# Reordering the second pass of the first batch in a fused attention and maxout-FFN kernel: left-over scores first, products on zeros, one AV moved

## The chip, the cores and the metric

The kernel runs on one core of one Trainium2 chip. The metric is device time in microseconds; the time before is the median of 11 runs, 325.95 us (323.8 to 327.2).

## What is computed

Attention with a relative position bias (the bias depends only on the distance of query and key and on the head), and after it a feed-forward network that takes the maximum of three products:

```python
# B, H, S, D = 8, 8, 576, 64;  d_model, d_ff = 512, 768
scores = scale * np.matmul(q, k.transpose(0, 1, 3, 2)) + bias
scores = scores - np.max(scores, axis=-1, keepdims=True)
attn = np.exp(scores)
attn = attn / (np.sum(attn, axis=-1, keepdims=True) + 1e-09)
x = np.matmul(attn, v)          # then (B * S, H * D) = (4608, 512)
h = np.maximum(np.maximum(x @ w1, x @ w2), x @ w3)
out = h @ w_out
```

## The kernel before

**Tiles.** Two heads make a pair, four pairs (`hp` = 0 to 3) a batch. Of 576 queries and keys, 512 are handled in four tiles of 128, and the left-over 64 of both heads of a pair together make one more tile. A pair's scores are computed transposed, keys on the partitions, and go through ACT's exponential into `e4` (512 keys by 512 queries, two heads) and `el` (left-over keys, and after them left-over queries). `visit(qT, kT, e4, c)` (L524) makes the scores of all four key tiles for the 256 queries of half `c`: two `sc` tiles, each four matmuls and one exponential of 1024 columns. `left_keys` (L540) makes the left-over keys' scores (`sct`), `left_queries` (L556) the left-over queries' (`scq`). DVE then multiplies the bias in as a factor: `times_band` (L512) on `e4`, `times_bandt` and `times_band_left` on `el` (together `products`, L713). `bandt` is a transposed copy of that factor, made once from `hank` by four DVE copies in `make_bandt` (L305).

**AV.** `attend(b, hp, e4, el, half)` (L572) multiplies the exponentials by the values for 256 queries of a pair, for half 1 also for the left-over queries. The values lie in `vx` (512 rows, four parts of one DMA each) and `vt` (left-over rows), each with a column of ones that gives the sum. It returns `quotients`, which divides on DVE and writes the rows to `x_sb`. In the first batch `x_transposes(hp, half)` (L622) turns these on PE into `xT` (copied by ACT), the operand of the FFN; later batches do it with DMA transposes (L619).

**Order in the first batch.** The first pass (L688) visits the four pairs for queries 0 to 255 and puts their half-0 AV in the list `late`. The second pass (L719) visits them for queries 256 to 511; each pair takes waiting AVs from `late` with `next_late()` (which issues the AV's products at once and returns the function that divides), and puts its own half-1 AV at the end. Before, pairs 0 and 1 take two AVs each, pairs 2 and 3 one each. `more_transposes(hp + 1)` (L481), between the two `sc` tiles of a visit, turns the next pair's queries on PE and copies them to `qT` on DVE. From the third pair on the FFN of the first 256 rows is there (`add_ffn(0, QS)`, L731): a list of pieces, which `fill(target, *hooks)` (L423) takes in order until their sizes reach `target` (one of 4 and one of 8 here), calling the hooks before the last piece. The three pieces of a 128-by-512 group in `ffn` are called f (first, copied by ACT), m (second) and g (third); f and m, g make portions of 4 and 8.

**Second batch.** Its q and k arrive packed (`load_packed`, L203), queued on POOL behind the FFN weights, and are spread by POOL for pair 0 (L210); `second_transposes(qk[1], 0)` (L490) turns them on PE. Then the main loop (L768) starts with `visit` of batch 1, pair 0. From batch 2 on, q and k are turned by DMA transposes on SP (L447).

**What fixes the order.** PE, DVE's marked instructions and the DMAs keep program order (`inorder`); the remaining ones are placed by the framework. PSUM tiles come in pairs: `ps_s` for scores, `ps_a` for AV and for `keep_warm`, `ps_f` for transposes and FFN. A product into a tile waits until the tile's earlier content is read. `keep_warm()` (L680) is one product of a block of zeros, 512 columns, whose result nobody reads; the first pass calls it once a pair.

The part of the second pass that the change rewrites, as it stands before (L744 to L764):

```python
        if hp < 2:
            quotients()
            keys()
            if hp == 1:
                x_transposes(1, 0)
            quotients = next_late()
            queries()
            quotients()
            ...
        else:
            ...
            quotients()
            late_bands()
            fill(8, keys, queries, *([lambda: second_transposes(qk[1], 0)] if hp == HP - 1 else []))
            products(hp, el)
```

Of the kernel before, what the change touches and what calls it, by code (L numbers as in the profile page):

```python
# [39 lines left out]
def kernel(  # L40
# [13 lines left out]
    B, H, S, D = q.shape  # L54
    d_model, d_ff = moe_w1.shape
    NB = bias_table.shape[0]
    P = 128
    assert d_model == H * D and S == 576 and D == 64 and NB == 32 and H == 8
    inv_sqrt_d = 1.0 / float(np.sqrt(D))
    HP = H // 2  # L60
    QS = 2 * P
# [31 lines left out]
    def mm(*args, **kw):  # L93
        inorder(nc.tensor.matmul(*args, **kw))  # L94

    def tr(*args):
        inorder(nc.tensor.transpose(*args))
# [3 lines left out]
    vx = [const.tile([P, KT, H, VW], BF16, name=f"vx{i}") for i in range(2)]  # L101
# [4 lines left out]
    def act_copy(out_, in_):  # L106
        return inorder(nc.scalar.activation(out=out_, in_=in_, func=ACTF.Copy))

    def dve_copy(out_, in_):
        return inorder(nc.vector.tensor_copy(out_, in_))  # L110

    def other_banks(later, earlier):

        for a in later:
            for b in earlier:
                tc.declare_no_dep(a.ins, b.ins, reason="they read different PSUM banks")
# [10 lines left out]
    def main_part(src, b):  # L127
        return src[b, :, 0 : KT * P, :].rearrange("h (t p) d -> p t h d", p=P)

    def tail_part(src, b, h0, h1, par):  # L130
        return src[b, h0 + par : h1 : 2, KT * P : S, :].rearrange("h p d -> p h d")

    def in_turn(b, load):
        return inorder(load) if b > 2 else load
# [27 lines left out]
    def load_qk(b, behind=None):  # L162

        loads = []
        for t in range(KT):
            for src, dst in zip((q, k), batch[b]):
                loads.append(in_turn(b, nc.gpsimd.dma_start(out=dst[:, t], in_=main_part(src, b)[:, t])))  # L167
        for src, dst in ((q, q_diag), (k, k_diag)):
            for par in range(2):
                load = nc.gpsimd.dma_start(out=dst(b, par, 0, H), in_=tail_part(src, b, 0, H, par))  # L170
                loads.append(in_turn(b, load))
        if behind:
            for load in loads:
                tc.add_manual_dep(
                    load.ins, behind.ins.name,
                    mybir.DependencyInfo(mybir.DependencyClass.Sync, mybir.DependencyReason.DATA),
                    reason="these loads go behind the result's transposes",
                )
# [33 lines left out]
    def load_tiles():  # L212
        q_sb = loads.tile([P, KT, H, D], BF16, tag="q_sb", name="q_sb")
        k_sb = loads.tile([P, KT, H, D], BF16, tag="k_sb", name="k_sb")
        return q_sb, k_sb

    batch = [None] * B
# [23 lines left out]
    zeros = xT[:, 1, NTOK - CH :]  # L241
# [63 lines left out]
    def make_bandt():  # L305
        for par in range(2):
            r = slice(64 * par, 64 * par + 64)
            c = BAND // 2 - 64 * par
            for c0, c1 in ((192, 256), (0, 192)):
                dve_copy(bandt[r, :, c0:c1], hank[r, par::2, c : c + c1 - c0][:, :, ::-1])  # L310
# [97 lines left out]
    def add_ffn(t0, nt, last=False):  # L408
        portions, left = ffn(t0, nt, last)
        portions[0] = rest + portions[0]  # L410
        rest[:] = left
        pending.extend((sum(n for n, _ in p), [fn for _, fn in p]) for p in portions)
# [10 lines left out]
    def fill(target, *hooks):  # L423

        groups, spent, hooks = [], 0, list(hooks)
        while pending and (not groups or spent + pending[0][0] <= target):
            n, fns = pending.pop(0)
            spent += n
            groups += [fn for fn in fns if fn]
        for j, group in enumerate(groups):  # L430
            while hooks and (j == len(groups) - 1 or j > 0 and len(hooks) > len(groups) - 1 - j):
                hooks.pop(0)()
            group()
        for hook in hooks:
            hook()
# [18 lines left out]
    def qk_tiles():  # L454
        return [qkt.tile([P, HP, (KT + 1) * P], BF16, tag=n, name=n) for n in ("qT", "kT")]
# [34 lines left out]
    def second_transposes(made, hp):  # L490

        hs = slice(2 * hp, 2 * hp + 2)
        tp = ps_s.tile([P, 2, 2 * CH], BF16, tag="sc", name="tp")
        for j, tl in enumerate((qtail, ktail)):
            for t in range(KT):
                tr(tp[:, j, P * t : P * t + P], batch[1][j][:, t, hs, :].rearrange("p h d -> p (h d)"), ident[:])
            tr(tp[:, j, KT * P : KT * P + P], tl[1][:, hp, :], ident[:])
        main = [
            copy(
                made[j][:, hp, 0 : KT * P].rearrange("c (p t) -> c p t", t=KT),  # L500
                tp[:, j, 0 : KT * P].rearrange("c (t p) -> c p t", t=KT),
            )
            for j, copy in enumerate((dve_copy, act_copy))
        ]
        tail = [
            copy(made[j][:, hp, KT * P :], tp[:, j, KT * P : (KT + 1) * P])
            for j, copy in enumerate((dve_copy, act_copy))
        ]
        other_banks([main[1], tail[1]], [main[0], tail[0]])
        other_banks([tail[0]], [main[1]])  # L510
# [40 lines left out]
    def times_bandt(hp, el):  # L551
        inorder(nc.vector.tensor_tensor(
            out=el[:, S - 192 : S + 64], in0=el[:, S - 192 : S + 64], in1=bandt[:, hp, :], op=ALU.mult
        ))
# [9 lines left out]
    def times_band_left(hp, el):  # L564
        last_tile = el[:, S + P * KT - 64 :].rearrange("p (h q) -> p h q", h=2)
        inorder(nc.vector.tensor_tensor(
            out=last_tile, in0=last_tile, in1=hank[:, 2 * hp : 2 * hp + 2, P - 64 : P][:, :, ::-1], op=ALU.mult,
        ))
# [53 lines left out]
    def x_transposes(hp, half):  # L622

        xp = ps_f.tile([P, 2 * CH], BF16, tag="ff", name="xp")
        lo, hi = (0, QS) if half == 0 else (QS, S)
        for q in range(lo // P, -(-hi // P))[::-1]:
            c = min(P * q, S - P) - lo
            tr(xp[:, c : c + P], x_sb[0][:, q, P * hp : P * hp + P], ident[:])
        act_copy(xT[:, hp, lo:hi], xp[:, 0 : hi - lo])
# [8 lines left out]
    def next_late():  # L638
        return late.pop(0)() if late else (lambda: None)

    def e_tiles():
        return (
            ep.tile([P, KT, 2, QM], BF16, tag="e4", name="e4"),
            ep.tile([P, S + 64 + KT * P], BF16, tag="el", name="el"),
        )
# [3 lines left out]
    qk = [qk_tiles(), qk_tiles()]  # L649
# [27 lines left out]
        for t in range(KT):  # L677
            times_band(hp, first_e[hp], t, 0, QS, inorder)

    def keep_warm():  # L680

        idle = ps_a.tile([P, CH], F32, tag="a", name="idle")
        mm(idle[:], lhsT=zeros[:, 0:P], rhs=zeros[:])


    first_e, lefts = [], []
# [1 line left out]
    for hp in range(HP):  # L688
        qT, kT = (x[:, hp, :] for x in qk[0])
        e4, el = e_tiles()  # L690
# [22 lines left out]
    def products(hp, el):  # L713
        times_bandt(hp, el)
        times_band_left(hp, el)
# [3 lines left out]
    for hp in range(HP):  # L719
        qT, kT = (x[:, hp, :] for x in qk[0])  # L720
        e4, el = e_tiles()
        visit(qT, kT, e4, 1, (lambda: more_transposes(hp + 1)) if hp + 1 < HP else None)
        if hp == 0:
            bands(HP - 2)
            bands(HP - 1)
        if hp == 1:
            x_transposes(0, 0)
        if hp == 2:
            x_transposes(2, 0)
            x_transposes(3, 0)  # L730
            add_ffn(0, QS)  # L731
        quotients = next_late()

        def keys():
            left_keys(hp, qT, kT, el, QS, S + 64)

        def queries():
            left_queries(hp, qT, kT, el)

        def late_bands():  # L740
            for t in range(KT):
                times_band(hp, e4, t, QS, QM, inorder)

        if hp < 2:  # L744
            quotients()
            keys()
            if hp == 1:
                x_transposes(1, 0)
            quotients = next_late()
            queries()  # L750
            quotients()
            if hp == 0:
                make_bandt()
            late_bands()
            products(hp, el)
        else:
            if hp == HP - 1:
                batch[2] = load_tiles()
                load_qk(2)
                x_transposes(0, 1)  # L760
            quotients()
            late_bands()
            fill(8, keys, queries, *([lambda: second_transposes(qk[1], 0)] if hp == HP - 1 else []))
            products(hp, el)  # L764
        late.append(lambda hp=hp, e4=e4, el=el: attend(0, hp, e4, el, 1))

    turned = [lambda hp=hp: x_transposes(hp, 1) for hp in range(1, HP)]
    for b, hp in [(b, hp) for b in range(1, B) for hp in range(HP)]:  # L768
# [3 lines left out]
        e4, el = e_tiles()  # L772
# [17 lines left out]
        quotients = next_late()  # L790
# [15 lines left out]
        quotients = next_late()  # L806
# [67 lines left out]
```

## Time and profile before

| | |
|---|---|
| median of 11 runs | 325.95 us (323.8 to 327.2) |
| profiled execution | 325.35 us, span 323.6 us, mean granted clock 0.987 |
| PE busy | 310.0 us (96% of the span) |
| DVE busy | 215.6 us (67%) |
| ACT busy | 202.3 us (63%) |
| POOL busy | 112.8 us (35%) |
| first AV of the first batch | starts at 20.36 us |
| first scores of the second batch | start at 37.00 us |

The span runs from the first to the last instruction of the execution; "busy" of PE includes time in which products are in the pipeline, so that 96% doesn't say that the array could not do more. The stage of the change lies between some 16 and 37 us: it is 5% of the span, and the shares of the whole span say little about it. Times below are from the start of the span.

### The profile page before, as it was taken

To read this page: it belongs to the slowest core of one execution; us is meant where nothing else is said; L and a number is where in the kernel's file an instruction comes from. 1 tells how busy PE (TensorE), PEld (TensorE's weight loads), DVE (VectorE), ACT (ScalarE), POOL (GpSimd) and SP (SyncE) were. 2 spreads that over 40 slices of the span, in tenths; PEclk is the share of its full clock that TensorE was granted. 3 is DMA by queue.
4 is the path that set the end of the run, shared out by engine and by line. 5 is a ranking of instruction groups with operands and counts; after the bars stand their busy time and mean duration, and the time that the engine had idled before them with its cause. 6 is when DMAs were issued, how large, how long until landed. Compare 5 with 4: busy or idle time off the path is not lost.

```text
span 323.6 us, 8019 instructions
## 1 busy us (share of the span) xinstructions
PE 310.0 (96%) x3232; PEld 176.1 (54%) x3232; DVE 215.6 (67%) x537; ACT 202.3 (63%) x274; POOL 112.8 (35%) x151
## 2 busy tenths in 40 slices
PE   7858999999999999999999999999999999999995
PEld 2336777776555555555555555555555554444442
DVE  6386778777667767676667676767767675454452
ACT  4868898898676677776777577767776751121221
POOL 8941886209847851295009600500000000000000
PEclk9789999999999999999999999999999999999998
DMA  9999999969999999999979997996032003301103
GB/s 169 176 200 196 147 154 151 169 139 142 191 158 155 164 198 163 92 143 188 169 88 119 176 209 71 112 201 116 1 75 99 33 3 75 131 0 65 67 0 130
DMA packets 165541, 40.72 MB, mean 126 GB/s; under 512 B 155384, under 2 KB 161024, under 8 KB 165504
## 3 DMA queue, kind: packets, MB, share of 16 engines
q0 software_dynamic: 103904, 16.66, 75.2%
q1 hardware_dynamic: 59840, 23.08, 37.9%
q10 hardware_dynamic: 1760, 0.47, 0.7%
q8 instruction: 25, 0.41, 0.5%
q14 instruction: 12, 0.10, 0.1%
HBM read 35.39 MB, written 9.45 MB: 139 GB/s over the span
## 4 chain that ended last, share of the span: by engine, by line
PE 77%; DMA 8%; SPq 3%; POOL 3%; ACT 3%; DVE 3%; issue 1%; POOLq 0%; ACTq 0%
PE ps L94 38%; PE a L94 14%; PE pso L94 13%; PE sc L94 8%; DMA kT<-k_sb 5%; SPq L447 3%; DMA vt<-in_v_dram 2%; PE sct L94 2%; ACT e L522 2%; PE scq L94 2%; DVE e L516 1%; POOL q_sb L143 1%; POOL vx L143 1%; DVE x_sb L609 1%; DMA out_dram<-osb 1%
## 5 line engine op out<-in xcount | busy, mean ns | idle before, releaser
L94 PE MATMUL ps<-xT,w_bf 128*128 128x512 bf16 (+1 forms) x720 | 155.7, 358 | 0.0
L522 ACT ACTIVATE e<-sc 128x1024 bf16<-128x1024 f32 x128 | 124.3, 1023 | 25.9 <-PE sc L94 25.2
L94 PEld LDWEIGHTS <-w_bf 128*128 128x128 bf16 x720 | 65.7, 98 | 56.8 <-issue 1.5
L516 DVE TENSOR_TENSOR e<-e,hank 128x512 bf16<-128x512 bf16 (+2 forms) x136 | 60.6, 474 | 26.1 <-ACT e L522 25.0
L337 ACT ACTIVATE m<-ps 128x512 bf16<-128x512 f32 x54 | 32.3, 598 | 65.5 <-PE ps L94 63.1
L343 DVE TENSOR_TENSOR m<-ps,m 128x512 bf16<-128x512 f32 x54 | 37.3, 691 | 45.8 <-ACT el L522 25.9
L94 PEld LDWEIGHTS <-kT 64*128 64x128 bf16 (+1 forms) x704 | 35.8, 96 | 39.6 <-issue 22.4
L94 PE MATMUL pso<-wo_bf,hT 128*128 128x512 bf16 (+2 forms) x222 | 51.0, 373 | 0.0
L94 PE MATMUL a<-vx,e 128*128 128x65 bf16 x1024 | 45.6, 194 | 0.0
L143 POOL DMA_DIRECT2D vx<-in_v_dram x32 | 28.3, 895 | 45.8 <-PE a L94 39.3
L94 PE MATMUL sc<-qT,kT 64*128 64x256 bf16 x512 | 41.8, 277 | 2.4 <-DVE kT L110 1.0
L94 PE MATMUL a<-vt,el 128*128 128x130 bf16 (+1 forms) x192 | 39.9, 215 | 3.0 <-DMA vt<-in_v_dram 3.0
L94 PEld LDWEIGHTS <-e 128*128 128x128 bf16 x1024 | 41.2, 98 | 0.9
L348 DVE TENSOR_TENSOR hT<-ps,m 128x512 bf16<-128x512 f32 x54 | 37.0, 686 | 5.2 <-PE ps L94 3.6
L609 DVE TENSOR_TENSOR x_sb<-a,rd 128x256 bf16<-128x256 f32 (+1 forms) x64 | 31.4, 491 | 2.2
L94 PEld LDWEIGHTS <-el 128*128 128x128 bf16 x448 | 24.2, 97 | 14.2 <-issue 9.7
L110 DVE COPY osb<-pso 128x512 f32<-128x512 f32 (+1 forms) x33 | 22.7, 688 | 13.4 <-PE pso L94 9.7
L94 PEld LDWEIGHTS <-hT 128*128 128x128 bf16 x222 | 20.2, 98 | 20.6 <-DVE hT L348 0.4
L167 POOL DMA_DIRECT2D q_sb<-in_q_dram x24 | 22.1, 922 | 15.2 <-DVE x_sb L609 12.7
L522 ACT ACTIVATE el<-sct 128x640 bf16<-128x640 f32 (+2 forms) x36 | 23.0, 643 | 4.1 <-PE sct L94 3.5
L167 POOL DMA_DIRECT2D k_sb<-in_k_dram x24 | 21.9, 913 | 3.8 <-DMA vx<-in_v_dram 2.5
L522 ACT ACTIVATE el<-scq 128x512 bf16<-128x512 f32 x32 | 19.0, 595 | 6.0 <-PE scq L94 6.0
(69 smaller groups left out, 168.4 us busy)
## 6 DMA issues: line engine op xcount, KB each, us to landing
out_dram<-osb SPq DMA_DIRECT2D x35, 256.0 KB, 2.7
vx<-in_v_dram POOLq DMA_DIRECT2D x32, 128.0 KB, 6.2
q_sb<-in_q_dram POOLq DMA_DIRECT2D x26, 128.0 KB, 8.0
k_sb<-in_k_dram POOLq DMA_DIRECT2D x24, 128.0 KB, 8.9
w_bf<-in_moe_w_dram POOLq DMA_DIRECT2D x3, 768.0 KB, 14.6
xT<-in_k_dram SPq DMA_DIRECT2D x6, 128.0 KB, 4.7
hank<-w_dr SPq DMA_DIRECT2D x2, 384.0 KB, 6.9
wo_bf<-in_moe_w_out_dram POOLq DMA_DIRECT2D x1, 768.0 KB, 7.8
```

Source lines behind the costliest of these rows:

```text
L94: inorder(nc.tensor.matmul(*args, **kw))
L110: return inorder(nc.vector.tensor_copy(out_, in_))
L143: in_turn(b, nc.gpsimd.dma_start(out=dst[:, t, h0:h1, :], in_=x[:, t, h0:h1, :]))
L167: loads.append(in_turn(b, nc.gpsimd.dma_start(out=dst[:, t], in_=main_part(src, b)[:, t])))
L337: nc.scalar.activation(out=st[fb]["m0"][:], in_=ps0, func=ACTF.Copy)
L343: inorder(nc.vector.tensor_tensor(out=m[:], in0=ps1, in1=st[fb]["m0"][:], op=ALU.max))
L348: inorder(nc.vector.tensor_tensor(out=hT[:, fb * CH : fb * CH + CH], in0=ps2, in1=st[fb]["m"][:], op=ALU.max))
L447: inorder(nc.sync.dma_start_transpose(out=made[j][:, :, P * t : P * t + P], in_=src))
L516: put(nc.vector.tensor_tensor(out=e4[:, t, :, lo:hi], in0=e4[:, t, :, lo:hi], in1=hank[:, 2 * hp : 2 * hp + 2, c0:c1][:, :, ::-1], op=ALU. ...
L522: nc.scalar.activation(out=out_, in_=in_, func=ACTF.Exp, scale=inv_sqrt_d)
L609: divided[b, hp, half] = inorder(nc.vector.tensor_tensor(out=x_sb[b][:, 2 * half : 2 * half + n, P * hp : P * hp + P].rearrange("p t (h d) ...
```

## The change

In the second pass each pair gets its own sequence.

- Pair 0: left-over keys and queries first; four products of zeros; two more of zeros by the third part of the values (these wait for that part to be loaded); then one AV and its division, then `make_bandt`. Before: AV, keys, AV, queries.
- Pair 1: three AVs instead of two; the keys behind the first, then `x_transposes(1, 0)`; the queries behind the second.
- Pair 2: AV, keys, queries, and only then `x_transposes(2, 0)`, `x_transposes(3, 0)` and `add_ffn`, which stood ahead of the AV. No FFN piece is taken here.
- Pair 3: the loads of batch 2 and `x_transposes(0, 1)` stand ahead of the AV; then keys, queries, four products of zeros, bands and left-over products; then `fill(16, ...)`, which takes the pieces f0, m0 with g0, and f1, with the second batch's transposes before f1. Before, f0 ran in pair 2, m0 and g0 in pair 3 with the transposes between them, and f1 in the second batch.

Everything after that takes FFN portions one place further on in the list. On DVE, the division of pair 1's AV now comes behind `make_bandt`, pair 0's bands and products and a `qT` copy.

```diff
-    def keep_warm():
+    def keep_warm(n=1, rhs=None):
 
         idle = ps_a.tile([P, CH], F32, tag="a", name="idle")
-        mm(idle[:], lhsT=zeros[:, 0:P], rhs=zeros[:])
+        for _ in range(n):
+            if rhs is None:
+                mm(idle[:], lhsT=zeros[:, 0:P], rhs=zeros[:])
+            else:
+                mm(idle[:].rearrange("p (h d) -> p h d", d=D), lhsT=zeros[:, 0:P], rhs=rhs)
...
+        if hp == 0:
+            keys()
+            queries()
+            keep_warm(4)
+            keep_warm(2, vx[0][:, 2, :, 0:D])
+            next_late()()
+            make_bandt()
+        elif hp == 1:
             x_transposes(0, 0)
+            quotients = next_late()
+            quotients()
+            keys()
+            x_transposes(1, 0)
+            quotients = next_late()
+            queries()
+            quotients()
+            next_late()()
+        elif hp == 2:
+            quotients = next_late()
+            keys()
+            quotients()
+            queries()
             x_transposes(2, 0)
             x_transposes(3, 0)
             add_ffn(0, QS)
...
+        else:
+            batch[2] = load_tiles()
+            load_qk(2)
+            x_transposes(0, 1)
+            quotients = next_late()
             quotients()
             keys()
             queries()
+            keep_warm(4)
+        late_bands()
+        products(hp, el)
+        if hp == HP - 1:
+            fill(16, lambda: second_transposes(qk[1], 0))
```

## What the change is expected to do

> **What bounds the kernel now.** I read the page's shares first (PE 96%), then the chain that ended last, then PE's timeline with windows of its clock for the stage that the change rewrites, the second pass of the first batch (from about 16 us to 37 us), and last DVE and POOL in that stage. After 66.2 us the list of waits has none of PE of 0.2 us or more, so whatever the change does to PE up to there reaches the end. Inside the stage PE is not the limit everywhere. First the start, in the chain of waits and in PE's timeline (start, us, instruction, idle before it and its releaser):
>
> ```profile
> 12.88 7.34 DMA vt<-in_v_dram
> 20.22 0.14 issue
> ...
> 20.36 0.22 PE L94 MATMUL a<-vt,el 128*128 128x130 bf16 x1 [3.04 <-DMA vt<-in_v_dram]
> ...
> 25.36 0.27 PE L97 MATMUL xp<-ident,x_sb 128*128 128x128 bf16 x2
> ...
> 29.25 0.27 PE L97 MATMUL xp<-ident,x_sb 128*128 128x128 bf16 x2 [1.50 <-ACT xT L107]
> ...
> 35.53 0.40 PE L97 MATMUL tp<-ident,k_sb 128*128 128x128 bf16 x4
> ...
> 37.00 0.62 PE L94 MATMUL sc<-qT,kT 64*128 64x256 bf16 x8
> ```
>
> PE stands still until the left-over values have landed (20.22), and the second batch's first scores start at 37.00. What holds that start is not PE but POOL, which waits for the weights' DMAs before it can spread the second batch's q and k:
>
> ```profile
> 33.08 0.82 POOL L205 DMA_DIRECT2D xT<-in_q_dram  x1 [3.11 <-DMA w_bf<-in_moe_w_dram]
> 34.03 0.69 POOL L210 COPY q_sb<-xT 128x512 bf16<-128x512 bf16 x1
> 34.66 0.81 POOL L210 COPY k_sb<-xT 128x512 bf16<-128x512 bf16 x1
> ```
>
> The copy of k ends at 35.47 and the transposes of k start at 35.53: every delay before that is free today, including these, cut by windows of 3.41 us (length, PE busy, instructions, granted clock, DMA, GB/s):
>
> ```profile
> 7.98:11.39 3.41, 2.19 (x20) 0.99 2.15 162
> 11.39:14.81 3.42, 3.42 (x25) 0.51 1.30 167
> 14.81:18.22 3.41, 1.98 (x22) 1.00 1.68 202
> 18.22:21.63 3.41, 1.27 (x34) 0.99 1.40 202
> 21.63:25.05 3.42, 3.42 (x43) 0.51 1.16 211
> 25.05:28.46 3.41, 2.62 (x45) 1.00 1.16 210
> ```
>
> The array ran at half clock from 21.63 to 25.05, the window after the idle one. And DVE, which the change reorders:
>
> ```profile
> 22.62 0.98 DVE L110 COPY bandt<-hank 64x256 bf16<-64x256 bf16 x4
> 23.64 0.96 DVE L516 TENSOR_TENSOR e<-e,hank 128x256 bf16<-128x256 bf16 x3
> ...
> 24.85 0.35 DVE L110 COPY qT<-tp 128x384 bf16<-128x384 bf16 x1
> 25.30 0.18 DVE L608 RECIPROCAL rd<-a 128x4 f32<-128x4 f32 x1
> 25.52 0.42 DVE L609 TENSOR_TENSOR x_sb<-a,rd 128x256 bf16<-128x256 f32 x1
> ```
>
> **What the Trainium skill says.** "TensorE: Matmul & The Clock Gate", Part 1, has the array's clock gated to half after an idle window of about 3.4 us, the windows free-running and not tied to the kernel's start. The trace agrees on length and grid: the cold stretches 11.39 to 14.81 and 21.63 to 25.05 are 3.42 us each and begin three windows apart. How little work counts as idle the trace leaves open: 1.27 of 3.41 us busy was followed by a cold window, 1.98 was not, but 2.19 was. The same page (Part 2, what each phase is for) lets weight loads run ahead while matmuls keep program order; so a transpose that waits for x_sb holds everything behind it, as 29.25 shows.
>
> **The change part by part.**
>
> *Gap before the values.* Pair 0's keys and queries go in front of AV. The score buffer of the keys is free when the first exponential ends (18.03: it starts at 17.02 and takes 1.02), that of the queries at 19.0. Then four zero products (0.216 us each, a quarter of the 0.86 us from one ps x4 row to the next), 19.28 to 20.14, and two on the third part of the values, to 20.58. These last wait for that DMA, and AV is queued behind them; AV could have started at 20.36, so it starts 0.22 late. The third part was issued before the left-over values and may land as late as they do (20.22), hence 0 to 0.45; I take 0.22. What leaves PE's work after 20.36 is keys 0.16 and queries 0.25. The window 18.22 to 21.63 is then busy for about 2.7 us instead of 1.27, so the cold stretch at 21.63 should go.
>
> *What is late next.* Only one AV now stands in pair 0, and the AV of pair 1 comes behind pair 1's scores. Its quotient therefore comes, in DVE's new order, behind the first quotient, the four band copies, the band products, the left-over products and a qT copy. With AV's start S this is: first reciprocal at S+0.80 (21.16 against 20.36), band copies 0.56 later, qT copy 2.23 after these begin (24.85 - 22.62), reciprocal 0.45 on (25.30 - 24.85), quotient done 0.64 on (25.52 + 0.42 - 25.30): S+4.68, or 25.26. x_transposes(1, 0) stands right behind pair 1's keys and needs that quotient. PE gets there after AV 0.60, scores 0.33, transposes 0.16, scores 0.33, transposes 0.12, AV 0.60, keys 0.17: 22.9. So PE stands about 2.4 us at full clock, with two AVs and the queries behind it. Before, the same transposes ran at 25.36, after one AV (0.60) more. What the warm clock gives is eaten here.
>
> *From there to the second batch,* warm: transposes 0.11, AV, queries, AV 1.5 to 26.9; pair 2's scores 0.82 to 27.75; AV of pair 0's second half 0.90 to 28.65. ACT's exponentials (0.97 each, 1.93 a pair) run 27.3 to 29.25; the queries wait for the second, 29.55. Four x transposes 0.24, pair 3's first scores 29.8, its second when the queries' exponential frees a buffer (29.25 + 0.40 + 0.55), 30.3 to 30.6; x transposes and AV 1.07 to 31.7; exponentials 30.85 to 32.8 behind two xT copies; the queries 32.85 to 33.1. Then on PE alone: four zeros 0.86 to 34.0, three FFN pieces of 0.87 to 36.6, the second batch's transposes 0.55 (POOL's copies long done), the piece f1 0.87 to 38.0. Scores of the second batch: 38.1, so 1.1 us later than 37.00. The 1.5 us wait at 29.25 is gone, but three short waits for exponentials and four zeros stand in its place.
>
> *What comes back.* f1 (0.87) is done ahead. The FFN pieces are one ahead from there on; PE's total is unchanged but for ten zeros. At 66.19 PE waited 0.20 for a transpose of batch 2 that landed at about 66.15; arriving later, it no longer does. Net when warm: 1.1 - 0.87 - 0.20 = 0.0.
>
> *Cold or warm after the new wait.* The window 21.63 to 25.05 would now be busy for about 1.4 us of 3.41, near the 1.27 that was followed by half clock. Then 25.05 to 28.46, where PE has work nearly throughout, loses half of 3.3, about 1.6 us, and nothing hides it, since 38.1 already lies past POOL's copies. The price is 0 to 1.6 us; the grid floats, so that some executions split the wait over two windows. I take 1.35.
>
> *Other queues.* POOL's order is unchanged. On SP one store (0.53 us at 82.18) now precedes the tail transposes of batch 2; PE needs them at least 1.1 us later too, so nothing. FFN rows of the second batch are wanted one piece earlier: their fourth transpose is issued at 73.14 and lands 4.8 later, 77.9, against 78.6 for the first product that needs it, both moved by the same delay. Margin 0.65; if it fails, up to 1 us.
>
> **The sum.** 0.0 + 1.35 = +1.35 us. Against the profiled execution, 325.35 us (span 323.6 and 1.75 around it), that is 326.7; this run lies 0.6 below the median 325.95, which gives 327.3.
>
> **The rivals.**
> - A: new wait, clock stays warm, +0.0, 326.0. For it: 1.98 busy did not gate. Against: 1.4 is far less.
> - B, the other side, faster: the wait at x_transposes(1, 0) is absorbed. ACT and DVE are ahead of PE when it ends, so that PE runs through to the second batch with few waits; scores start at about 37.0 with f1 done: -0.87 - 0.20, 324.9. It decides if the stretch from 25.3 to those scores is at most 11.9 us and warm. For it: before needed 11.64 with 1.85 us of waits in it. Against: this stretch gains an AV, f1 and four zeros, 2.35 us.
> - C: the transposed rows come late in batch 2 on top of the cold stretch: +2.3, 328.3. For it: the margin of 0.65. Against: both sides move together.
> - D: the zeros don't keep the clock up. Then 21.63 to 25.05 is cold, but DVE's chain still sets 25.3; costs nothing beyond A.
>
> **How the numbers follow.** Likeliest (wait and cold stretch) 0.48, A with D 0.26, B 0.20, C 0.06. Low end: B's 324.9 less 0.1; high end: the full 1.6, the 0.45 of the zeros and C in part, 328.6. The likeliest case alone: 326.6 to 328.0. A measurement of this kernel tells about 0.3%, 1.0 us, from no change. Likeliest: 0.42 slower, 0.06 same; A: 0.19 same, 0.04 slower, 0.03 faster; B: 0.17 faster, 0.03 same; C slower. Faster 0.20, same 0.28, slower 0.52.
>
> **What would show it.** Right: no half clock at 21.6; PE idle about 2.4 us before the xp transposes at 25.3, released by DVE x_sb; half clock in the window after; the second batch's first scores at 39 or later; no wait at 66. Wrong: those scores at 37.2 or sooner, or the quotient of pair 1 ready before 24.

## The result, and the profile after

The changed kernel takes 329.87 us in the median of 12 runs (327.21 to 332.24), the kernel before, run beside it, 325.89 us (47 runs). The ratio is 1.0115 with a 95% interval of 1.0092 to 1.0138; this ratio and those below are formed from the executions within 1.5% of the fastest of their kernel and so are not the quotients of the medians beside them. That is slower by 3.7 us, where 1.35 us had been forecast, and 329.87 us lies past the upper end of the range. The profiled execution took 329.84 us (span 328.0), 4.5 us over that of before.

First the stage that the change rewrites: PE's timeline of the kernel after (start, us, instruction, idle before it and its releaser).

```profile
18.80 1.90 PE L94 MATMUL idle<-xT 128*128 128x512 bf16 x4
20.49 1.06 PE L94 MATMUL idle<-vx,xT 128*128 128x512 bf16 x2
21.34 0.32 PE L94 MATMUL a<-vt,el 128*128 128x130 bf16 x1
...
24.09 0.32 PE L94 MATMUL sct<-qT,kT 128*128 128x384 bf16 x1
26.30 0.29 PE L97 MATMUL xp<-ident,x_sb 128*128 128x128 bf16 x2 [1.89 <-DVE x_sb L609]
...
34.03 1.03 PE L94 MATMUL idle<-xT 128*128 128x512 bf16 x4
...
39.05 0.62 PE L94 MATMUL sc<-qT,kT 64*128 64x256 bf16 x8
```

The forecast wait stands where it was put, ahead of the turning of pair 1's rows, 1.89 us long. The same kernel's DVE timeline shows why: the second reciprocal and quotient come behind the band copies, the products and a qT copy.

```profile
22.55 0.18 DVE L608 RECIPROCAL rd<-a 128x4 f32<-128x4 f32 x1 [1.22 <-PE a L94]
...
23.11 0.98 DVE L110 COPY bandt<-hank 64x256 bf16<-64x256 bf16 x4
...
25.34 0.35 DVE L110 COPY qT<-tp 128x384 bf16<-128x384 bf16 x1
25.61 0.18 DVE L608 RECIPROCAL rd<-a 128x4 f32<-128x4 f32 x1
25.82 0.42 DVE L609 TENSOR_TENSOR x_sb<-a,rd 128x256 bf16<-128x256 f32 x1
```

The clock did not do what was forecast. Windows of the kernel after (length, PE busy, PEld, DVE, ACT, POOL, granted clock, DMA share, GB/s):

```profile
15.49:18.90 3.41, 1.71 (x17) 1.06 (x18) 1.42 (x5) 3.41 (x6) 1.06 (x3) 0.99 1.65 227
18.90:22.31 3.41, 3.41 (x25) 1.76 (x23) 2.43 (x9) 0.61 (x2) 2.47 (x4) 0.51 1.20 209
22.31:25.72 3.41, 2.10 (x39) 1.27 (x35) 3.09 (x13) 2.60 (x4) 0.53 (x1) 1.00 1.16 210
25.72:29.13 3.41, 2.83 (x61) 2.26 (x62) 2.15 (x8) 1.74 (x3) 0.30 (x2) 1.00 1.16 210
```

The zeros that were to keep the clock up lie themselves in the half-clock window 18.90 to 22.31, and the window after the new wait runs at full clock. The second batch's scores begin at 39.05, 2.05 after those of before; 0.87 of it is f1, done early. That leaves 1.2 us, against 4.5 in the whole execution: most of the loss arises after this stage. The same stretches of 34 us show where. Before:

```profile
70.00:104.00 34.00, 33.90 (x403) 20.29 (x400) 24.30 (x60) 25.44 (x34) 24.44 (x31) 1.00 1.81 153
104.00:138.00 34.00, 34.00 (x371) 18.76 (x368) 23.80 (x57) 23.76 (x31) 15.86 (x21) 1.00 1.65 153
138.00:172.00 34.00, 34.00 (x370) 18.78 (x368) 23.74 (x57) 23.75 (x31) 14.39 (x19) 1.00 1.47 141
```

After:

```profile
70.00:104.00 34.00, 33.13 (x380) 19.43 (x377) 23.54 (x59) 24.74 (x33) 22.48 (x28) 1.00 1.66 141
104.00:138.00 34.00, 32.87 (x364) 18.19 (x362) 23.09 (x55) 23.56 (x30) 15.53 (x21) 1.00 1.96 160
138.00:172.00 34.00, 33.51 (x367) 18.52 (x366) 23.34 (x55) 23.45 (x30) 14.29 (x18) 1.00 1.64 136
```

PE, busy throughout before, now stands still in each. The list of waits of the kernel after, PE from 40 us on (us in total, times, longest), names what for:

```profile
PE sc L94 <- DMA kT<-k_sb: 1.6, 2, 1.1
PE sct L94 <- ACT e L522: 0.6, 3, 0.2
PE ps L94 <- DMA xT<-x_sb: 0.5, 1, 0.5
...
PE sct L94 <- DMA kT<-ktail: 0.2, 1, 0.2
```

These add to 2.9 us; before had 0.4 of these kinds, one wait of 0.20 for exponentials and the one of 0.20 for kT at 66.19. The two waits for kT stand at 136.25 and 170.80, in the first scores of batches 4 and 5 (numbered from 0 as in the code, so that the second batch is batch 1): their DMA transposes came late. They are issued on SP one batch ahead. SP's queue in batch 3, before (first scores of the batch at 95.63):

```profile
98.13 8.47 SPq L619 DMA_TRANSPOSE xT<-x_sb  x5
106.71 1.20 SPq L447 DMA_TRANSPOSE qT<-q_sb  x1
108.43 1.19 SPq L447 DMA_TRANSPOSE kT<-k_sb  x1
109.73 0.52 SPq L379 DMA_DIRECT2D out_dram<-osb  x1
...
119.96 1.72 SPq L447 DMA_TRANSPOSE kT<-k_sb  x1
```

And after (first scores of the batch at 100.74):

```profile
103.23 8.94 SPq L619 DMA_TRANSPOSE xT<-x_sb  x5
112.27 1.57 SPq L379 DMA_DIRECT2D out_dram<-osb  x1
114.38 1.31 SPq L447 DMA_TRANSPOSE qT<-q_sb  x1
115.79 1.21 SPq L447 DMA_TRANSPOSE kT<-k_sb  x1
...
126.95 2.75 SPq L447 DMA_TRANSPOSE kT<-k_sb  x1
```

Because the FFN portions are taken one place earlier, a finished output tile is waiting one visit earlier, and `store_outputs()` puts its store in front of the batch's first transposes. Counted from the batch's first scores, the first qT transpose is issued at 13.64 instead of 11.08, and the issue of the last kT of a full tile ends at 28.96 instead of 26.05. The next batch's scores begin 8.1 us after that end in the kernel before and 4.9 us in the kernel after. How long the kT transposes between 120 and 140 us took from their issue to their landing in the kernel after:

```profile
DMA to landing us min/median/max: 6.6/8.0/8.9
```

By the end of the queue it is no longer the one store that makes the difference: in both kernels four stores stand ahead of the last transposes of a full tile. Of the 2.9 us at the end, 1.6 are the four kT transposes, which hold SP for 7.47 us in all instead of 5.89, and 0.7 the four stores (3.10 instead of 2.36). This is a reading of one execution each. Whether the order on SP, the later start or the zeros carry the loss is what the experiments ask.

### The profile page after: what moved, and what is told of

It reads as the page before. It is cut to its first block, busy times and chain, and to the rows that moved or that the text cites. A ratio compares the mean times of both kernels' runs of the same rounds, so it can differ in the third digit from the quotient of the medians.

```text
span 328.0 us, 8041 instructions
## 1 busy us (share of the span) xinstructions
PE 312.2 (95%) x3242; PEld 176.4 (54%) x3242; DVE 215.6 (66%) x537; ACT 202.2 (62%) x274; POOL 112.7 (34%) x151
## 4 chain that ended last, share of the span: by engine, by line
PE 59%; DMA 19%; ACT 8%; POOL 5%; SPq 3%; issue 3%; DVE 2%; POOLq 0%; ACTq 0%
PE ps L94 30%; PE pso L94 9%; PE a L94 9%; DMA q_sb<-in_q_dram 6%; ACT e L522 6%; PE sc L94 6%; DMA k_sb<-in_k_dram 3%; SPq L447 3%; DMA kT<-k_sb 3%; DMA kT<-ktail 2%; DMA xT<-x_sb 2%; PE scq L94 2%; DMA ktail<-in_k_dram 2%; PE sct L94 2%; POOL vx L143 1%
## 5 line engine op out<-in xcount | busy, mean ns | idle before, releaser
L516 DVE TENSOR_TENSOR e<-e,hank 128x512 bf16<-128x512 bf16 (+2 forms) x136 | 60.6, 473 | 27.9 <-ACT e L522 25.8
L94 PE MATMUL sc<-qT,kT 64*128 64x256 bf16 x512 | 41.0, 272 | 3.7 <-DMA kT<-k_sb 1.6
L94 PEld LDWEIGHTS <-hT 128*128 128x128 bf16 x222 | 20.1, 97 | 20.3 <-DVE hT L348 0.4
```

Of the source, the lines that this page charges most:

```text
L516: put(nc.vector.tensor_tensor(out=e4[:, t, :, lo:hi], in0=e4[:, t, :, lo:hi], in1=hank[:, 2 * hp : 2 * hp + 2, c0:c1][:, :, ::-1], op=ALU. ...
```

## The experiments

All ratios are to the kernel before, run beside each of them, with 95% intervals; the difference of two of them carries both intervals, and is known to some 0.3 to 0.4%. "Lead" stands for f1 in the first batch, with all later FFN portions one place ahead.

**The lead taken out of the changed kernel** (f1 back in the second batch):

```diff
-            fill(16, lambda: second_transposes(qk[1], 0))
+            fill(12, lambda: second_transposes(qk[1], 0))
```

> The changed kernel with f1 left to the second batch (the last fill of the first batch takes 12 instead of 16), so that every FFN portion is again in the place where the kernel before has it; all else as changed. Theory P (the portions one place ahead cost time in every later batch, by what they put ahead of the DMA transposes on SP and by wanting transposed rows earlier): the second batch's scores start at about 38.2 us, 1.2 late, and the delay does not grow from there, no wait of 0.4 us for a DMA transpose at the start of batches 4 and 5: 326.7 to 327.3 us, ratio 1.003 to 1.005. Theory L (the late start alone puts the batches out of step with their loads, whatever the FFN's place): the waits stay and the ratio is 1.009 to 1.012. The forecast on record (only the second pass costs, the later part is PE's): as the changed kernel, 329.9, or up to 0.2 less.

1.0038 (1.0017 to 1.0060), 327.38 us. Two thirds of the loss go with the lead; 0.4% stay. As expected, its profile has no wait for a DMA transpose at the start of batches 4 and 5, but one of 1.07 us for kT at 97.49, at the start of batch 3: such waits are not the lead's alone.

**The lead alone, put into the kernel before:**

```diff
-            fill(8, keys, queries, *([lambda: second_transposes(qk[1], 0)] if hp == HP - 1 else []))
+            fill(12 if hp == HP - 1 else 8, keys, queries, *([lambda: second_transposes(qk[1], 0)] if hp == HP - 1 else []))
```

> The kernel before with one thing changed: the last fill of the first batch takes 12 instead of 8, so f1 runs there and every later FFN portion is one place ahead, as in the changed kernel. Nothing in the second pass ahead of it is touched. Theory P: slower by 1 to 2.5 us, ratio 1.003 to 1.008, with a wait for a DMA transpose of keys at the start of a later batch. Theory L and the forecast on record: f1 is done ahead but the second batch starts 0.87 later, so no change, 0.998 to 1.002.

1.0090 (1.0064 to 1.0116), 329.06 us. The second pass is that of before, and yet most of the loss is here. That the rewritten pass ends late can't be the main cause.

**The order on SP.** In both visits of the main loop the store goes behind the transposes, first in the changed kernel:

```diff
         visit(qT, kT, e4, 0)
-        store_outputs()
         if b == 1:
             ...
             next(crossbar)
+        store_outputs()
         early()
```

> The changed kernel, but in each visit from batch 1 on the next batch's DMA transposes are issued ahead of the stores that are due, which gives SP the order of the kernel before; the FFN portions stay one place ahead. Theory P, in the form that the store ahead of the first transposes is what costs: the waits of 1.1 us at the start of batch 4 and of 0.5 to 0.7 at batch 5 go, 328.0 to 328.5 us, ratio 1.006 to 1.008. If the portions cost by the rows that they want earlier, or by their place on PE: as the changed kernel, 1.010 to 1.013. Theory L: no change either.

1.0092 (1.0061 to 1.0122), 329.24 us: it gives back 0.2%, which can't be told from nothing. In its profile PE's wait at the start of batch 4 fell from 1.13 to 0.20 us and the one at the start of batch 5 is gone, but 0.88 us of wait for kT of the left-over keys came at 208.00. The same edit on the kernel before with the lead, and on the kernel before alone:

> The kernel before with f1 run in the first batch (all FFN portions one place ahead), and with each visit's DMA transposes issued ahead of its stores, which gives SP the order of the kernel before. With the portions ahead and SP's order as it came, the ratio was 1.009. If the store in front of the first transposes is what makes the portions' lead dear: 1.003 to 1.005, what is left being the wait for transposed rows in batch 2 (0.7 us) and three waits of 0.2 us for exponentials. If the lead costs through the moments at which loads and transposes meet, whatever SP's order: 1.007 to 1.010.

1.0025 (1.0003 to 1.0048), 326.64 us.

> The kernel before with each visit's DMA transposes issued ahead of its stores, the FFN where it was. SP's order of stores and transposes is then one store later than in the kernel before. If SP's order is what decides how early the transposes are: the last transposes of a batch are issued up to 2 us earlier, the waits of 0.2 to 0.3 us at the start of batches 2 and 3 can shrink: 0.996 to 1.000. If SP's order doesn't matter: 0.999 to 1.001.

1.0002 (0.9980 to 1.0024), 325.24 us. So the edit is worth nothing by itself, and of the lead's 0.90% it takes away 0.65, more than the two intervals leave to noise. The order on SP carries most of what the lead costs in this kernel. What stays is 0.25%, 0.8 us. The waits of that profile are more than this: 0.9 us for the rows turned by DMA, three times 0.2 us for exponentials and 0.5 us for kT.

**The new wait.** x_transposes(1, 0) moved behind pair 1's third AV:

```diff
             keys()
-            x_transposes(1, 0)
             quotients = next_late()
             queries()
             quotients()
             next_late()()
+            x_transposes(1, 0)
```

> The changed kernel with the x transposes of pair 1 moved behind pair 1's third AV, so that the second AV and the queries no longer stand behind the division of the first; DVE's order stays. The third AV needs that division too, for its buffer. So of the 1.9 us of wait about 0.9 should go. Forecast on record and theory P both: the second batch starts 0.9 us earlier, at about 38.1; if later parts only follow, 329.0 us, ratio 1.008 to 1.010. If the loss arises after the second batch's start alone, the total stays at 1.011 to 1.013.

1.0123 (1.0088 to 1.0158), 330.12 us. No gain can be seen. But the run tests less than the whole wait: 1.22 us of it came back in front of the third AV (at 27.66), which waits for the same division, so that some 0.67 us went, 0.2%, and the interval is wider than that. Where the rest of the wait would show in the total, this run doesn't say.

**The AV moved back.** The kernel without the lead, with two AVs in pair 0 and two in pair 1, as before:

```diff
             next_late()()
+            next_late()()
             make_bandt()
...
             quotients()
-            next_late()()
```

> The changed kernel with f1 left to the second batch and with the AV of pair 1 and its division back in pair 0, behind the first. The x transposes of pair 1 then find their rows ready; zeros, left-over scores first and the rest as changed. The second pass was 0.7 us late without this (scores of the second batch at 37.66 in one profile). All theories of the second pass: the wait of 1.5 us at those transposes goes, the second batch starts at 36.9 to 37.2, limited by POOL's copies; ratio 0.999 to 1.003, against 1.0038 with the AV moved.

1.0037 (1.0014 to 1.0060), 327.28 us, where the same kernel with one AV moved has 1.0038. The move of the AV can't be seen in the total, where the difference of the two is known to 0.3%.

**The zeros.** The kernel without the lead and without the ten products of zeros:

```diff
             keys()
             queries()
-            keep_warm(4)
-            keep_warm(2, vx[0][:, 2, :, 0:D])
             next_late()()
...
             queries()
-            keep_warm(4)
```

> The changed kernel with f1 left to the second batch and without the ten products of zeros of the second pass. If the zeros in pair 0 keep the array at full clock, the half clock now falls into the AVs and scores of pair 1 and the second batch starts later than 37.7, ratio 1.004 to 1.007. If they do nothing for the clock and only take time (0.2 us ahead of AV, 0.9 in pair 3): the second batch starts 0.6 to 0.9 us earlier, at about 37.0, ratio 1.000 to 1.003.

1.0010 (0.9985 to 1.0036), 326.48 us: of the 0.38% that stayed, the zeros are 0.28 by these two ratios, a difference that alone is within noise. In its profile the second batch begins at 35.79, 1.2 us ahead of before, and nothing of that is seen at the end. PE's timeline of this run, at the start of batch 2:

```profile
64.28 0.50 PE L94 MATMUL sc<-qT,kT 64*128 64x256 bf16 x6
66.39 0.28 PE L94 MATMUL sc<-qT,kT 64*128 64x256 bf16 x2 [1.61 <-DMA kT<-k_sb]
```

The scores wait for a transpose that lands at about 66.4; before, they waited for it 0.20 us at 66.19. SP's queue has no store ahead of it in either kernel.

The zeros did change the clock, which one profile alone doesn't show. Over the executions that the ratios use, the mean granted clock of the six kernels with pair 0's zeros is 0.993 to 0.995 (the changed kernel: 0.994), that of the kernel before and the seven without them 0.989 to 0.991. An estimate from this: 0.004 of 326 us are 2.6 us less at half clock in an execution, most of one stretch of 3.4. In the total no gain from it is seen.

**Zeros of pair 0 or of pair 3.** The four of pair 3 alone left out, those of pair 0 kept, no lead (the diff is the last line of the one above):

> The changed kernel with f1 back (fill 12) and with the zeros of pair 0 kept, those of pair 3 (four products, 0.86 us) left out. Theory the zeros of pair 3 stand on PE's own path and those of pair 0 hide in the wait for the values: 1.0038 - 0.0026 = 1.001, about 326.3 us, start of the second batch at about 36.8 or below. Rival, the zeros of pair 0 delay AV (they ran at half clock and ended 1.0 us past the values) and carry the loss: 1.0038 stays within 0.1%, 327.1 us.

1.0014 (0.9992 to 1.0036), 326.95 us. The step from 1.0038 is 0.24%, 0.8 us, near what four zeros take on PE (0.86), though alone it is within noise. Pair 0's six zeros cost 0.04%, which can't be told from nothing; in this profile they lie in the wait for the values (AV still waits 1.48 us behind them), in that of the changed kernel they don't. The second batch begins at 38.05, not at 36.8 or below. Two windows of this run show the half clock that the forecast expected after the new wait, and that the profiled execution of the changed kernel didn't have:

```profile
22.40:25.81 3.41, 1.52 (x30) 1.06 (x31) 3.05 (x13) 2.37 (x4) 0.61 (x1) 1.00 1.16 209
25.81:29.22 3.41, 3.41 (x49) 2.85 (x45) 1.30 (x5) 1.17 (x3) 0.83 (x1) 0.50 1.16 209
```

**The parts together.** The lead without the zeros, in the order on SP that the change makes:

> The changed kernel, fill 16, SP's order as it came, without the ten products of zeros. Theory the zeros are 0.28% wherever they stand: 1.0115 - 0.0028 = 1.0087, about 328.7 us, start of the second batch's scores at about 37.2. Rival, the lead's loss comes from transposes that are issued at times set by SP and not by PE, so an earlier PE only waits longer: 1.0115 again within 0.2%, about 329.6 us, with more waits for qT, kT or xT from the third batch on. Rival, the zeros carry the whole rest of the loss: 1.004 or less, 327.2 us.

1.0086 (1.0052 to 1.0119), 329.18 us. The same with the transposes ahead of the stores:

> The changed kernel, with f1 kept in the first batch (fill 16), without the ten products of zeros of the second pass, and with the DMA transposes issued on SP ahead of the output store in each visit. Theory parts add (the lead costs 0.65% through SP's order in the kernel before, the zeros 0.28% at fill 12): 1.0115 - 0.0065 - 0.0028 = 1.002 of before, about 326.6 us. Rival, order of SP gives back only what it gave in the changed kernel with zeros (0.23%): 1.0064, about 328.0 us. Rival, the lead fills the wait of 1.61 us for kT at 66.39 that stood in the run without zeros at fill 12, so that the earlier start is kept: 0.998 or less, under 325.3 us, with no wait over 0.5 us near 66.

1.0025 (0.9999 to 1.0052), 327.00 us. And that without the lead:

> The changed kernel with f1 back in the second batch (fill 12), without the ten products of zeros, and with the DMA transposes ahead of the stores on SP. Theory the wait of 1.61 us for kT at 66.39 is due to loads and transposes that have no store ahead of them in the second batch: unchanged, 1.001 of before, about 326.3 us. Rival, the order of stores and transposes makes it: the wait falls under 0.5 us and the earlier start by 1.2 us is kept, 0.997, about 324.9 us.

0.9990 (0.9968 to 1.0011), 325.93 us, not to be told from the kernel before. The wait of 1.61 us at the start of batch 2 is gone from its profile, though the transposes stand in the same order there in both runs: the issue of that kT held SP for 2.54 us in the one and for 1.22 in the other, and PE comes 0.74 us later here (scores at 65.02 instead of 64.28; the second batch, up to which the two are the same, at 36.54 instead of 35.79). So neither the order on SP nor a fixed landing time explains that wait; that it returns in each execution is not shown.

PE's waits in the first of these three runs:

```profile
135.01 0.28 PE L94 MATMUL sc<-qT,kT 64*128 64x256 bf16 x2 [1.65 <-DMA kT<-k_sb]
...
170.06 0.28 PE L94 MATMUL sc<-qT,kT 64*128 64x256 bf16 x2 [0.99 <-DMA kT<-k_sb]
```

And in the second:

```profile
135.28 0.28 PE L94 MATMUL sc<-qT,kT 64*128 64x256 bf16 x2 [0.66 <-DMA kT<-k_sb]
...
206.72 0.45 PE L94 MATMUL sct<-qT,kT 128*128 128x512 bf16 x2 [0.51 <-DMA kT<-ktail]
```

2.64 us of waiting for k have become 1.17; with the wait in the FFN of the second batch, 0.76 there and 0.52 here, that is 1.7 us less in one execution of each, beside 2.0 us (0.61%) between the ratios. (The wait of 0.76 is put down to DVE's copy of an output tile, that of 0.52 to the rows turned by DMA.)

How the order does this is only in part to be seen. SP's queue in batch 3 of the first of the two (first scores of the batch at 98.97):

```profile
110.51 0.52 SPq L379 DMA_DIRECT2D out_dram<-osb  x1
111.56 2.54 SPq L447 DMA_TRANSPOSE qT<-q_sb  x1
...
125.14 3.08 SPq L447 DMA_TRANSPOSE kT<-k_sb  x1
```

And of the second (first scores at 100.24):

```profile
111.79 1.19 SPq L447 DMA_TRANSPOSE qT<-q_sb  x1
...
126.30 2.74 SPq L447 DMA_TRANSPOSE kT<-k_sb  x1
```

The first transpose is issued 12.59 and 11.55 us after the batch's start, and the last one of a full tile ends at 29.25 and 28.80, where the kernel before had 26.05. In this batch the order gives back 0.45 us at the end of the queue, and most of the lateness stays with the order restored; in batch 4, which begins with the waits above, the ends are at 29.71 and 27.40. Why the transposes hold SP longer with the lead was not tried; that they meet other transfers is one possibility.

| | f1 in the second batch | f1 ahead |
|---|---|---|
| second pass of before | 1 | 1.0090 |
| the same, transposes ahead of stores | 1.0002 | 1.0025 |
| changed pass without zeros | 1.0010 | 1.0086 |
| the same, transposes ahead of stores | 0.9990 | 1.0025 |
| changed pass, zeros in pair 0 alone | 1.0014 | |
| changed pass with all zeros | 1.0038 | 1.0115 (the change) |
| the same, transposes ahead of stores | | 1.0092 |

Read across, the lead costs 0.76% without zeros and 0.77% with them; read down, the zeros cost 0.28% without the lead and 0.29% with it. The two values for the zeros are each within noise, and together just outside it. As far as these intervals tell, the parts add. The last row fits least: with the order on SP worth 0.61 to 0.65% elsewhere, it should be about 1.005, under the lower end of its interval (1.0061), but with the intervals of both sides the gap of 0.4% may be noise. Whether the order gives back less there stays open; the wait of 0.88 us for left-over keys was seen in its profile, but not shown to be a reason.

## Why the prediction was wrong

The direction was right; the size and the main reason were not. Step by step:

- **The gap before the values.** Six zeros were put at 0.22 us. In the profiled execution they ran at half clock (the four took 1.69 us from start to the next row) and AV began 0.98 later than before. In the total pair 0's zeros cost 0.04%, so the small price holds within noise. That they hold the clock up is right on average, by the mean granted clocks above, but not in the way forecast: in this execution the half clock moved onto them.
- **The new wait at x_transposes(1, 0).** Right in place and cause: the quotient was forecast 4.68 us after AV's start and the transposes ran at 4.96, after 1.89 us of idle time where 2.4 had been forecast. The stretch from AV to the second batch's scores took 17.71 us, and 17.52 (38.1 less 20.58) had been forecast for the warm clock; that these agree so closely is in part luck, since AV's first products still ran at half clock. (The line at 29.25, which the forecast gave as a transpose waiting for x_sb, waits for ACT's copy of xT; what it shows, that everything behind it is held up, is the same.)
- **The cold stretch after it, +1.35.** The whole forecast loss stood on this term, and it did not occur in the profiled execution: the window with the wait had 2.10 us of PE work, not 1.4, because AV and with it all that follows lay elsewhere on the grid. It did occur in the run with pair 0's zeros alone (1.52 us busy, then half clock), which is at 1.0014 nevertheless. How often it occurs in the changed kernel is open; in the profiles of three runs with the same zeros (f1 back, the order on SP, x_transposes moved) the half clock again lies across the zeros, beginning between 19.3 and 20.1, and not behind the wait. The changed pass without the lead costs 0.38%, 1.2 us, almost the +1.35 of the sum. This is luck: by the ratios above most of it goes with the zeros, and no part of it was shown to come from the clock.
- **"PE's total is unchanged but for ten zeros."** PE's work is the same but for these zeros, and four of them, pair 3's, were counted on PE's path at 0.86 and cost about 0.8 us. But the lead is not free on account of it. It costs 0.77%, 2.5 us, the largest part of the loss, and in the forecast's sum it stood at nothing.
- **"On SP one store (0.53 us) ... so nothing."** The step that failed. It priced one store ahead of the tail transposes of batch 2, by its length, and let PE move with it. From batch 3 on a store stands ahead of the first transposes of each batch, whose last ones then end up to 2.9 us later, and PE waits for them. Putting these transposes ahead of the stores took away 0.61 and 0.65%, some 2 us, in two kernels with the lead, and nothing (1.0002) in the kernel before. That store's length is not the price: it held SP for 1.57 us in batch 3 of the changed kernel, but for 0.52 in its batches 4 and 5, and for 0.52 in batch 3 of the run without the zeros, where the lead costs the same. By which path the order costs so much stays open.
- **Rival C, the turned rows late in batch 2.** The margin of 0.65 us was used up: 0.48 us of wait at 81.71. A wait is there, 0.5 to 0.9 us, in all other runs with the lead but one (that with x_transposes moved), whatever the order on SP, so that it seems to belong to what the lead costs beyond SP's order; in the run with the lead and without zeros the profile puts it down to DVE's copy of an output tile. The forecast gave this rival 0.06.
- **"No wait at 66."** Right in the changed kernel, which arrives there late. The run without zeros, which arrived early in its profile, shows what can lie below: its earlier start of 1.2 us ended in a wait of 1.61.

## What to carry to other kernels

An edit that takes work one place earlier from a list moves more than that work: follow every queue through one whole period of the steady state, and not only the stage that was edited. Where a store and a transfer that something waits for share a queue, try the latter first: here it was worth 0.6% in two kernels with the lead, and nothing where no store stood ahead of the first transposes. A shift on the queue is to be read at the last transfer of the period; the length of the instruction that was put in (0.52 us) doesn't give its price. Before an earlier start is counted as a gain, look up which transfer the next stage waits for.

## What the runs showed of the hardware

- A DMA transpose holds SP for at least 1.19 us, and for up to 3.49 us in these runs; fifteen of them and four stores keep the changed kernel's queue of batch 3 occupied nearly without a gap from 103.23 to 132.32 us, of a batch of 33.9. The same transpose at the same place took 1.22 us in one run and 2.54 in another. What a reordering does at the head of so full a queue is not what it does at its end: 1.04 us and 0.45 in batch 3 of the two runs above.
- How much work in a window keeps the clock up can't be read from the busy time alone. The Trainium skill ("TensorE: Matmul & The Clock Gate", Part 1) speaks of an idle window of about 3.4 us; here 1.52 and 1.71 us of PE work in 3.41 were followed by half clock, 2.10 was not. Together with the kernel before (1.98 not, 2.19 followed by half clock) no limit on busy time fits all of them.
- Six products of zeros ran at half clock in one execution (four took 1.69 us) and at full clock in another (0.87 us, in the run with pair 0's zeros alone). In the first they began at 18.80, together with the half-clock stretch; in the second at 18.10, and no such stretch came before 25.8. Over the executions of each kernel the mean granted clock is 0.993 with pair 0's zeros alone and 0.989 without zeros, and the ratios (1.0014 and 1.0010) show no gain in time from it.
